# Keeping the FFN activation in PSUM for its first 26 steps: a fused gated-attention and FFN kernel on one core

## The chip, the cores and the metric

The kernel runs on one core of a Trainium2 chip (trn2). The time is device microseconds for one launch, the median of several executions. One execution was also taken with the profiler; its rows stand below. The engines are called as the profile calls them: PE (TensorE matmuls), PEld (its weight loads), DVE (VectorE), ACT (ScalarE), POOL (GpSimd), SP (SyncE, which issues the DMAs).

## The reference

Two parts run one after the other. The first is a gated linear recurrence over 768 time steps, for 4 batches of 8 heads with 48 features each; its output is the input of the second, an FFN over 3072 tokens (384 to 2048 to 384) with a piecewise activation.

```
for t in range(S):
    state = alpha[:, :, t, :, None] * state + einsum('bhd,bhe->bhde', k[:, :, t], v[:, :, t])
    y[:, :, t] = einsum('bhd,bhde->bhe', q[:, :, t], state)
x = y.transpose(0, 2, 1, 3).reshape(B * S, H * D)
h = x @ w_in
g = where(h >= 1, h, where(h <= -1, 0, (h + 1) ** 2 / 4))
out = g @ w_out
```

## The kernel before

**Attention.** The 3072 tokens are cut into 24 chunks of 128. For each chunk, `prepare` loads a, k, q and v and forms scaled queries and keys on DVE with two scans along the tokens (L549, L575), two multiplies (L591, L601; L601 is on POOL for most chunks) and small operations. `attend` runs the chunk's matmuls (L665, L678, L691, L818), updates the state (L720, and L795 on POOL) and writes the chunk's output to `ring` as a high and a low part (`end_chunk`: cast on ACT L842, subtraction on DVE L847).

**FFN.** Three chunks form a group, so there are eight groups of 384 tokens; 2048 hidden features are 16 blocks of 128. One *step* is one block of one group, 128 steps in all. The steps of the first two groups are taken in halves (group 0 blocks 0 to 7, group 1 blocks 0 to 7, group 0 blocks 8 to 15, group 1 blocks 8 to 15), so that the first eight blocks of weights serve two groups before the others are needed. A step's number in that order is its `key`. The very first step is cut in three parts of one chunk each.

A step is `hidden` and then `second`. `hidden` makes nine matmuls (L915) into a PSUM bank `h` of 128x384, then the activation: ACT takes relu(h/2 + 1/2) into the SBUF tile `gf` and squares it there (both L944); DVE takes max(min(gf, 1), h) into `gf` (L955); ACT casts `gf` to the high part `gh[:, 0]` (L961); POOL subtracts that from `gf` to give the low part `gh[:, 1]` (L962). The planner may give that subtraction to DVE instead, at a penalty. `second` makes nine matmuls (L980) from `gh` and the block of `w_out` into three output banks, `LAG` steps behind. For the very last step the subtraction is on DVE.

**Weights.** They are loaded as 64-bit words and decoded into a high and a low part for `w_in` and `w_out`, in units of two blocks: on ACT L367, L375, L420; on DVE L383, L394; on POOL L407, L422 (each with DVE as the second choice). That work falls in the first 145 us. The scratch tile `w` has two buffers. The part for `w_out` is due `LAG` steps after that for `w_in`.

**Order of the work.** Nothing is left to a run-time scheduler: `Plan.order` is a list scheduler that runs before the launch. Each operation has an engine, a written duration, a key (its due time in steps), dependencies and buffers. The scheduler goes forward in planned time; on each engine the operation that can start first goes next, the lower key first among those that can start at the same time. The result is a fixed order on each engine, and an engine that waits for one instruction holds up all behind it. Its PSUM is eight banks: at most two for `h` in planned time, three for the output, the rest for attention. An operation marked `port` may not start on DVE inside a planned `port` operation of POOL, or the other way round; `held` remembers that operation's planned start and end. The lines that do it:

```
        held = {"DVE": (0.0, 0.0), "POOL": (0.0, 0.0)}
                    if port:
                        a, b = held["POOL" if engine == "DVE" else "DVE"]
                        t = b + 0.05 * (engine == "DVE") if a <= t < b else t
            t, o, i = best
            o.start = t
            if o.port:
                held[o.engine] = (o.start, t)
```

In planned gaps of PE in the first 165 us the scheduler puts matmuls on zeros (`fill`, L1051), which do no work of the reference.

Of the kernel before, what the change touches and what calls it, by code (L numbers as in the profile page):

```python
# [30 lines left out]
PLACING = 4.0  # L31
MORE = 2
WARM = 15
LAG = 4.0
FETCH = 12.0
LOAD = 4.0
DECODE = 3.0
# [14 lines left out]
HELP = 4  # L52
SPLIT = 1
NEAR = 0.0


class Buf:
# [20 lines left out]
class Plan:  # L78
# [57 lines left out]
    def order(self):  # L136
        free = {"PE": 1.0, "DVE": 1.0, "ACT": 1.0, "POOL": 4.6, "SP": 0.8}
        slots = {name: [(0.0, -i, None) for i in range(n)] for name, (n, share, _) in self.sizes.items() if share == name}
        live = {name: 0 for name in self.sizes}
        left = {}  # L140
        for i, o in enumerate(self.ops):
            o.rank, o.left = i, len(o.deps)
            for d in o.deps:
                d.next.append(o)
            for b in o.allocs:
                left[b] = [len(b.users), 0.0]
        ready = {}
        for o in self.ops:
            if not o.left:
                self.offer(ready, o)  # L150
        mode, wire, done, freed = None, 0.0, [], 0
        held = {"DVE": (0.0, 0.0), "POOL": (0.0, 0.0)}
        while any(ready.values()):
            best = None
            for engine, waiting in ready.items():
                could = []
                for o, i in waiting:
                    _, _, key, _, port = o.ways[i]
                    t = max(free.get(engine, 0.0), o.ready)
                    need = {}  # L160
                    for b in o.allocs:
                        need[b.pool, b.early] = need.get((b.pool, b.early), 0) + 1
                    if any(
                        len(slots[self.sizes[p][1]]) < n or live[p] + n > self.sizes[p][2 if early else 0]
                        for (p, early), n in need.items()
                    ):
                        continue
                    for (p, _), n in need.items():
                        t = max(t, sorted(slots[self.sizes[p][1]])[n - 1][0])
                    if o.moved > 0:  # L170
                        t = max(t, wire - self.DEPTH)
                    if port:
                        a, b = held["POOL" if engine == "DVE" else "DVE"]

                        t = b + 0.05 * (engine == "DVE") if a <= t < b else t
                    could.append((t, key, o.rank, o, i))
                if not could:
                    continue
                soon = min(c[0] for c in could) + NEAR
                _, _, t, o, i = min((key, rank, t, o, i) for t, key, rank, o, i in could if t <= soon)  # L180
                if best is None or t < best[0]:
                    best = t, o, i
            assert best, "no instruction can go: " + str([(e, o.key, [b.pool for b in o.allocs], {p: len(x) for p, x in slots.items()}) for e, w in ready.items() for o, _ in w][:4])
            t, o, i = best
            for j, way in enumerate(o.ways):
                ready[way[0]].remove((o, j))
            o.engine, o.us, _, o.emit, o.port = o.ways[i]
            o.start = t
            rest = t - free["PE"]
            if o.engine == "PE" and self.REST < rest and 1.0 < t < WARMTH and slots["ps"] and min(slots["ps"])[0] <= free["PE"]:  # L190
                n = int((rest - 0.25) / self.FILL)
                f = Op("PE", n * self.FILL, o.key, lambda n=n: self.fill(n), False, "full", 0)
                f.start, f.end = free["PE"], free["PE"] + f.us
                mode = "full"
                done.append(f)
            if o.engine == "PE" and mode != o.mode:
                t += self.MODE
                mode = o.ends
            t += o.us
            free[o.engine] = t  # L200
            if o.port:
                held[o.engine] = (o.start, t)
            if o.moved > 0:
                wire = max(wire, t) + o.moved / self.RATE
                t = wire + self.LAND
            else:
                t += self.HOP.get(o.engine, 0.08)
            o.end = t
            done.append(o)
            for b in o.allocs:  # L210
                live[b.pool] += 1
                free_at = slots[self.sizes[b.pool][1]]
                taken = min(free_at)
                free_at.remove(taken)
                if taken[2]:
                    o.deps.update(taken[2].users)
            for b in o.uses:
                left[b][0] -= 1
                left[b][1] = max(left[b][1], t)
                if not left[b][0]:  # L220
                    live[b.pool] -= 1
                    freed += 1
                    slots[self.sizes[b.pool][1]].append((left[b][1], freed, b))
            for x in o.next:
                x.left -= 1
                x.ready = max(x.ready, t if x.engine != o.engine or o.moved else free[o.engine])
                if not x.left:
                    self.offer(ready, x)
        assert len(done) >= len(self.ops)
        return done  # L230
# [3 lines left out]
def gated_attention_ffn(ctx: ExitStack, tc: tile.TileContext, q, k, v, alpha, laid, out):  # L234
# [77 lines left out]
    with ExitStack() as main:  # L312
# [589 lines left out]
        def hidden(n, f, key, c0=0, c1=GROUP):  # L902

            c1 = min(c1, groups[n])
            L = (c1 - c0) * CH
            h = bank("ps_h", 2, [P, L])
            gf, gh = buf("fw", "gf", [P, L], 4), buf("fw", "gh", [P, 2, L], 4, F32R)
            xs = [("x", j % (2 * GROUP)) for j in range(first[n] + c0, first[n] + c1)]
            at = slice(span(n).start + c0, span(n).start + c1)

            def product():
                m = 0
                for kt in range(KT):
                    for w, a in ((0, 0), (0, 1), (1, 0)):
                        nc.tensor.matmul(  # L915
                            out=h(),
                            lhsT=win(f, w)[:, kt],
                            rhs=ring[:, at, kt, a, :],
                            start=(m == 0),
                            stop=(m == 3 * KT - 1),  # L920
                        )
                        m += 1


            firsts[:] = [
                plan.op(
                    "PE",
                    (0.529 if c1 - c0 > 1 else 0.7) * (c1 - c0),
                    key,
                    product,  # L930
                    [*xs, ("moved", n), wi[f // NW]],
                    [h],
                    mode="full",
                    after=firsts,
                )
            ]


            w = (c1 - c0) / GROUP
            act = lambda in_, func, scale, bias: plan.op(  # L940
                "ACT",
                0.08 + 0.45 * w,
                key + 0.4,
                lambda: nc.scalar.activation(out=gf(), in_=in_(), func=func, scale=scale, bias=bias),  # L944
                [h, gf] if in_ is gf else [h],
                [gf],
            )

            act(h, AF.Relu, 0.5, half_b)
            act(gf, AF.Square, 1.0, 0.0)  # L950
            plan.op(
                "DVE",
                0.08 + 0.45 * w,
                key + 0.4,
                lambda: nc.vector.scalar_tensor_tensor(  # L955
                    out=gf(), in0=gf(), scalar=1.0, in1=h(), op0=ALU.min, op1=ALU.max
                ),
                [gf, h],
                [gf],
            )  # L960
            plan.op("ACT", 0.08 + 0.41 * w, key + 0.4, lambda: nc.scalar.copy(out=gh()[:, 0], in_=gf()), [gf], [gh])  # L961
            sub = lambda e: e.tensor_tensor(out=gh()[:, 1], in0=gf(), in1=gh()[:, 0].bitcast(F32), op=ALU.subtract)  # L962
            ends = (n, f) == (NG - 1, NF - 1)
            ways = [("POOL", 0.1 + 0.9 * w, lambda: sub(nc.gpsimd), True), ("DVE", 0.08 + 0.45 * w, lambda: sub(nc.vector), True)]
            (e, us, emit, port), other = reversed(ways) if ends else ways
            plan.op(e, us, key + 0.4, emit, [gf, gh], [gh], port=port, other=None if ends else other)
            return gh

        o_ps, seconds, firsts = {}, {}, []
# [310 lines left out]
```

## Time and profile before

| | us |
|---|---|
| median of 3 runs | 522.08 (521.63 to 522.26) |
| profiled execution, its own time | 520.75 |
| span of the profiled execution, first to last instruction | 519.0 |
| mean granted TensorE clock | 0.99 |

The profiled execution's 520.75 us is its span and 1.75 us around it. PE is busy 498.3 us of the span, DVE 315.9, ACT 310.4, POOL 274.9. These are sums over stages with different limits, so the sections that follow read them by stretch. The work of DVE, ACT and POOL is heaviest in the first 145 us.

### The profile page before, as it was taken

Reading aid. Unit: us, or ns where it says so; the run is one execution under the profiler, and the core shown is the slowest. Engines: PE = TensorE matmul, PEld = TensorE weight load, DVE = VectorE, ACT = ScalarE, POOL = GpSimd, SP = SyncE. Lnnn points to the kernel's source line nnn. Section 1 sums busy time; section 2 is a strip of 40 time slices with the busy share of each in tenths; the row PEclk is TensorE's granted clock in tenths of the full one; section 3 lists DMA queues with packets and bytes.
Section 4 is the critical chain, followed back from the end, with each engine's and each line's share of the span. In section 5 each row is a group of like instructions: output and inputs, shape, how many; then the busy total and the mean of one; then the engine's idle time right before and its main releaser. Section 6 shows DMA issues by size and latency. Waiting matters only on the chain.

```text
span 519.0 us, 12190 instructions
## 1 busy us (share of the span) xinstructions
PE 498.3 (96%) x4820; PEld 480.2 (93%) x4820; DVE 315.9 (61%) x566; ACT 310.4 (60%) x607; POOL 274.9 (53%) x287
## 2 busy tenths in 40 slices
PE   9899999697999999999999999999999999999996
PEld 7778889696899999999999999999999999999995
DVE  6999999969696685467276456458358413112112
ACT  3898887665656555556555564556556555555541
POOL 3678887999953454455355354365365332333330
PEclk9999999978999999999999999999999999999999
DMA  8996958112226552454334452453222300001001
GB/s 261 375 348 195 317 168 330 43 57 82 71 70 166 157 163 57 113 135 122 81 115 99 119 147 59 111 128 113 56 53 63 79 29 14 11 3 45 1 1 51
DMA packets 59487, 59.81 MB, mean 115 GB/s; under 512 B 33601, under 2 KB 43297, under 8 KB 59425
## 3 DMA queue, kind: packets, MB, share of 16 engines
q1 hardware_dynamic: 59424, 58.97, 38.4%
q8 instruction: 40, 0.66, 0.5%
q14 instruction: 23, 0.18, 0.1%
HBM read 47.32 MB, written 9.57 MB: 110 GB/s over the span
## 4 chain that ended last, share of the span: by engine, by line
PE 73%; DVE 15%; issue 4%; POOL 3%; ACT 2%; DMA 1%; SPq 0%; DVEq 0%; POOLq 0%
PE ps L915 32%; PE ps L980 32%; PE ps L818 4%; DVE inv L575 2%; PE ps L691 2%; DVE Q L549 2%; PE ps L678 2%; DVE w L394 2%; DVE w L383 2%; DMA wt<-in_laid_w_in 1%; POOL gh L962 1%; DVE gf L955 1%; DVE Q L764 1%; POOL w L407 1%; DVE inv L591 1%
## 5 line engine op out<-in xcount | busy, mean ns | idle before, releaser
L962 POOL TENSOR_TENSOR gh<-gf,gh 128x384 fp32r<-128x384 f32 (+1 forms) x128 | 143.6, 1123 | 167.7 <-ACT gh L961 165.9
L980 PE MATMUL ps<-wt,gh 128*128 128x384 f32 x1152 | 226.3, 341 | 5.1 <-DVE gf L955 4.0
L915 PE MATMUL ps<-ring,wt 128*128 128x384 f32 (+1 forms) x1170 | 226.2, 338 | 1.6 <-DVE inv L575 1.2
L980 PEld LDWEIGHTS ps<-wt,gh 128*128 128x128 f32 x1152 | 202.4, 189 | 7.7 <-DVE gf L955 4.6
L915 PEld LDWEIGHTS ps<-ring,wt 128*128 128x128 f32 x1170 | 205.5, 189 | 2.6 <-ACT gf L944 1.5
L955 DVE SCALAR_TENSOR_TENSOR gf<-gf,ps 128x384 f32<-128x384 f32 (+1 forms) x130 | 70.1, 542 | 161.4 <-ACT gf L944 152.6
L961 ACT CAST gh<-gf 128x384 fp32r<-128x384 f32 (+1 forms) x130 | 65.8, 508 | 96.1 <-DVE gf L955 95.1
L944 ACT ACTIVATE gf<-ps,half_b 128x384 f32<-128x384 f32 (+1 forms) x130 | 74.8, 575 | 75.3 <-PE ps L915 71.9
L944 ACT ACTIVATE gf<-gf 128x384 f32<-128x384 f32 (+1 forms) x130 | 67.6, 520 | 4.0
L795 POOL TENSOR_TENSOR state<-state,last 128x192 f32<-128x192 f32 x20 | 20.1, 1006 | 33.1 <-DVE state L720 30.9
L407 POOL TENSOR_TENSOR w<-w,wt 128x384 int32<-128x384 int32 (+1 forms) x24 | 31.1, 1307 | 11.0 <-DVE w L394 5.1
L575 DVE TENSOR_TENSOR_SCAN inv<-raw,bwd 128x511 f32<-128x511 f32 x17 | 32.5, 1911 | 0.0
L422 POOL TENSOR_TENSOR wt<-w,wt 128x384 fp32r<-128x384 f32 (+1 forms) x25 | 31.3, 1266 | 1.9 <-ACT wt L420 1.7
L601 POOL TENSOR_TENSOR Q<-Q,raw 128x512 f32<-128x512 f32 x18 | 29.9, 1662 | 2.4 <-POOL last L558 1.0
L764 DVE TENSOR_TENSOR Q<-ps,mask 64x256 f32<-64x256 f32 x48 | 20.3, 423 | 15.2 <-ACT other L728 14.3
L818 PE MATMUL ps<-other,both 128*64 128x64 f32 x372 | 27.8, 229 | 0.2 <-DVE other L764 0.2
L818 PE MATMUL ps<-Q,both 128*64 128x64 f32 x372 | 27.9, 229 | 0.0
L818 PEld LDWEIGHTS ps<-Q,both 128*64 128x64 f32 x372 | 24.4, 141 | 2.7 <-issue 1.1
L710 ACT COPY both<-state 48x192 f32<-48x192 f32 x67 | 23.4, 349 | 2.6 <-DVE state L718 0.8
L549 DVE TENSOR_TENSOR_SCAN Q<-raw,fwd 128x512 f32<-128x512 f32 x17 | 24.4, 1434 | 0.8 <-PE ps L818 0.7
L818 PEld LDWEIGHTS ps<-other,both 128*64 128x64 f32 x372 | 24.3, 141 | 0.3 <-issue 0.3
L691 PEld LDWEIGHTS ps<-vt,ks 64*64 64x64 f32 x704 | 13.7, 138 | 9.5 <-ACT ks L668 5.3
(77 smaller groups left out, 411.2 us busy)
## 6 DMA issues: line engine op xcount, KB each, us to landing
both<-in_laid_v_both SPq DMA_DIRECT2D x48, 128.0 KB, 2.8
wt<-in_laid_w_in SPq DMA_DIRECT2D x8, 768.0 KB, 7.9
wt<-in_laid_w_out SPq DMA_DIRECT2D x8, 768.0 KB, 8.3
vt<-in_laid_v SPq DMA_DIRECT2D x24, 192.0 KB, 2.8
out<-ot SPq DMA_DIRECT2D x24, 192.0 KB, 1.9
raw<-in_laid_dim_a SPq DMA_DIRECT2D x17, 256.0 KB, 3.1
raw<-in_laid_dim_k SPq DMA_DIRECT2D x17, 256.0 KB, 3.4
raw<-in_laid_dim_q SPq DMA_DIRECT2D x17, 256.0 KB, 2.6
```

The lines of the kernel that those rows point to most:

```text
L407: add = lambda e, c=c: e.tensor_tensor(out=bits()[:, c], in0=bits()[:, c], in1=word(I32, 0)[:, c], op=ALU.add)
L422: sub = lambda e, c=c: e.tensor_tensor(out=part(1)[:, c], in0=data()[:, c], in1=part(0).bitcast(F32)[:, c], op=ALU.subtract)
L549: lambda: nc.vector.tensor_tensor_scan(flat(Q()), aT(), flat(fwd), 0.0, ALU.mult, ALU.max),
L575: lambda: nc.vector.tensor_tensor_scan(flat(inv())[:, 0:n][:, ::-1], aT()[:, 1 : n + 1][:, ::-1], flat(bwd)[:, 0:n][:, ::-1], bwd[:, G - 1 ...
L601: mul = lambda e: e.tensor_tensor(out=flat(Q()), in0=flat(Q()), in1=qT(), op=ALU.mult)
L818: nc.tensor.matmul(out=ps()[halves[r], to, halves[u]], lhsT=lhsT[:, r, u], rhs=x()[:, g, halves[u]], start=m + u == 0, stop=True, skip_gro ...
L915: nc.tensor.matmul(out=h(), lhsT=win(f, w)[:, kt], rhs=ring[:, at, kt, a, :], start=(m == 0), stop=(m == 3 * KT - 1),)
L944: lambda: nc.scalar.activation(out=gf(), in_=in_(), func=func, scale=scale, bias=bias),
L955: lambda: nc.vector.scalar_tensor_tensor(out=gf(), in0=gf(), scalar=1.0, in1=h(), op0=ALU.min, op1=ALU.max),
L961: plan.op("ACT", 0.08 + 0.41 * w, key + 0.4, lambda: nc.scalar.copy(out=gh()[:, 0], in_=gf()), [gf], [gh])
L962: sub = lambda e: e.tensor_tensor(out=gh()[:, 1], in0=gf(), in1=gh()[:, 0].bitcast(F32), op=ALU.subtract)
L980: nc.tensor.matmul(out=o_ps[seg][t](), lhsT=gh()[:, a, (t - c0) * CH : (t - c0 + 1) * CH], rhs=wout(f, w), start=(f == f0 and i == 0), sto ...
```

## The change

For the steps whose key is below `APART = 26` (the first part-steps of step 0 included) `x` is the PSUM bank `h` itself: DVE's max writes back into `h`, ACT casts out of it, and DVE, with no second choice, subtracts out of it. From step 26 on the chain is as before. `held` keeps the last four `port` operations of each engine instead of the last one, and each is tested. `LAG` goes from 4 to 3, for `second` and for the decoding of `w_out`.

```
-LAG = 4.0
+LAG = 3.0
+APART = 26.0
...
-        held = {"DVE": (0.0, 0.0), "POOL": (0.0, 0.0)}
+        held = {"DVE": [], "POOL": []}
...
-                        a, b = held["POOL" if engine == "DVE" else "DVE"]
-                        t = b + 0.05 * (engine == "DVE") if a <= t < b else t
+                        for a, b in held["POOL" if engine == "DVE" else "DVE"]:
+                            t = b + 0.05 * (engine == "DVE") if a <= t < b else t
...
-                held[o.engine] = (o.start, t)
+                held[o.engine] = [*held[o.engine][-3:], (o.start, t)]
...
+            x = h if key < APART else gf
             plan.op(
                 "DVE", 0.08 + 0.45 * w, key + 0.4,
                 lambda: nc.vector.scalar_tensor_tensor(
-                    out=gf(), in0=gf(), scalar=1.0, in1=h(), op0=ALU.min, op1=ALU.max
+                    out=x(), in0=gf(), scalar=1.0, in1=h(), op0=ALU.min, op1=ALU.max
                 ),
                 [gf, h],
-                [gf],
+                [x],
             )
-            plan.op("ACT", 0.08 + 0.41 * w, key + 0.4, lambda: nc.scalar.copy(out=gh()[:, 0], in_=gf()), [gf], [gh])
-            sub = lambda e: e.tensor_tensor(out=gh()[:, 1], in0=gf(), in1=gh()[:, 0].bitcast(F32), op=ALU.subtract)
+            plan.op("ACT", 0.08 + (0.45 if x is h else 0.41) * w, key + 0.4, lambda: nc.scalar.copy(out=gh()[:, 0], in_=x()), [x], [gh])
+            sub = lambda e: e.tensor_tensor(out=gh()[:, 1], in0=x(), in1=gh()[:, 0].bitcast(F32), op=ALU.subtract)
             ends = (n, f) == (NG - 1, NF - 1)
+            if x is h:
+                plan.op("DVE", 0.08 + 0.45 * w, key + 0.4, lambda: sub(nc.vector), [x, gh], [gh])
+                return gh
             ways = [("POOL", 0.1 + 0.9 * w, lambda: sub(nc.gpsimd), True), ("DVE", 0.08 + 0.45 * w, lambda: sub(nc.vector), True)]
             (e, us, emit, port), other = reversed(ways) if ends else ways
-            plan.op(e, us, key + 0.4, emit, [gf, gh], [gh], port=port, other=None if ends else other)
+            plan.op(e, us, key + 0.4, emit, [x, gh], [gh], port=port, other=None if ends else other)
             return gh
```

## Rows read from the trace of the kernel before

**Rows 1.** Busy time of each engine by stretch, in us from the start of the span: the stretch and its length, then for each engine busy us and the count of instructions, then the mean granted TensorE clock (1.00 is 2.4 GHz, 0.5 is 1.2 GHz), the busy share of the DMA engines and GB/s.

```profile
core 0: us, PE busy (x) PEld busy (x) DVE busy (x) ACT busy (x) POOL busy (x), PEclk, DMA share, GB/s
0.00:20.00 20.00, 18.32 (x274) 15.12 (x275) 15.19 (x34) 10.12 (x22) 9.48 (x23) 1.00 0.91 304
20.00:80.00 60.00, 55.17 (x768) 49.29 (x767) 56.96 (x105) 53.54 (x102) 48.44 (x58) 1.00 0.81 273
80.00:145.00 65.00, 55.78 (x460) 53.69 (x459) 54.35 (x70) 42.17 (x79) 57.23 (x41) 0.92 0.30 103
145.00:165.00 20.00, 19.76 (x198) 19.27 (x198) 15.11 (x27) 12.23 (x26) 8.52 (x11) 1.00 0.44 128
165.00:505.00 340.00, 340.00 (x3077) 334.27 (x3076) 170.65 (x326) 189.67 (x376) 150.19 (x155) 1.00 0.31 81
...
102.00:109.00 7.00, 5.98 (x103) 5.74 (x104) 4.34 (x5) 2.21 (x4) 6.92 (x6) 0.51 0.19 60
...
126.00:129.50 3.50, 3.50 (x13) 3.50 (x13) 3.43 (x6) 2.61 (x6) 3.50 (x3) 0.51 0.93 273
```

**Rows 2.** The order of PE's instructions from 94 to 126 us: start, length, engine, line, operation, names, shape, count, and in brackets the idle time before them and what ended it.

```profile
96.77 1.50 PE L980 MATMUL ps<-wt,gh 128*128 128x384 f32 x7 [1.07 <-POOL gh L962]
98.11 1.74 PE L915 MATMUL ps<-ring,wt 128*128 128x384 f32 x9
103.02 1.10 PE L691 MATMUL ps<-vt,ks 64*64 64x48 f32 x32 [3.18 <-ACT ks L668]
...
118.94 1.74 PE L915 MATMUL ps<-ring,wt 128*128 128x384 f32 x9
120.52 1.21 PE L980 MATMUL ps<-wt,gh 128*128 128x384 f32 x6
125.32 0.78 PE L980 MATMUL ps<-wt,gh 128*128 128x384 f32 x3 [3.60 <-DVE gf L955]
```

**Rows 3.** The chain that ended last, its pieces in order of time between 80 and 145 us: start, length, what. Only the pieces of L962 on POOL and the longer ones of L383, L394, L549 and L558 are shown.

```profile
82.46 1.31 DVE w L383
83.79 1.94 DVE w L394
...
94.81 1.91 POOL gh L962
...
99.94 1.28 POOL gh L962
...
101.30 1.24 POOL last L558
...
103.86 1.71 POOL gh L962
...
116.22 1.97 DVE w L383
...
118.21 1.66 DVE w L394
...
120.33 2.63 DVE Q L549
...
128.56 1.51 DVE w L383
...
136.28 1.72 POOL gh L962
```

**Rows 4.** Groups of POOL's instructions from 80 to 145 us: line, engine, operation, names, shapes, count, then busy us and mean ns of one, then idle time before them.

```profile
L962 POOL TENSOR_TENSOR gh<-gf,gh 128x384 fp32r<-128x384 f32 x16 | 21.8, 1365 | 1.3 <-ACT gh L961 1.3
```

**Rows 5.** The same groups of DVE from 80 to 145 us.

```profile
L394 DVE SCALAR_TENSOR_TENSOR w<-wt,w 128x768 int32<-128x768 int32 x8 | 12.0, 1502 | 0.2
L383 DVE TENSOR_SCALAR w<-w 128x768 int32<-128x768 int32 x8 | 10.7, 1332 | 0.8 <-ACT w L367 0.8
L549 DVE TENSOR_TENSOR_SCAN Q<-raw,fwd 128x512 f32<-128x512 f32 x3 | 6.4, 2140 | 0.0
L575 DVE TENSOR_TENSOR_SCAN inv<-raw,bwd 128x511 f32<-128x511 f32 x3 | 6.2, 2079 | 0.0
```

**Rows 6.** The same groups from 20 to 80 us, two of POOL and then four of DVE.

```profile
L962 POOL TENSOR_TENSOR gh<-gf,gh 128x384 fp32r<-128x384 f32 x6 | 8.2, 1386 | 0.5 <-ACT gh L961 0.4
...
L962 POOL TENSOR_TENSOR gh<-gf,gh 128x128 fp32r<-128x128 f32 x3 | 2.4, 799 | 0.0
...
L575 DVE TENSOR_TENSOR_SCAN inv<-ps,bwd 128x511 f32<-128x511 f32 x5 | 6.4, 1272 | 0.0
L549 DVE TENSOR_TENSOR_SCAN Q<-ps,fwd 128x512 f32<-128x512 f32 x5 | 6.1, 1223 | 0.2
...
L962 DVE TENSOR_TENSOR gh<-gf,gh 128x384 fp32r<-128x384 f32 x1 | 0.8, 804 | 0.2 <-ACT gh L961 0.2
L955 DVE SCALAR_TENSOR_TENSOR gf<-gf,ps 128x128 f32<-128x128 f32 x3 | 0.8, 278 | 0.0
```

**Rows 7.** Single instructions of DVE in order of time, at moments when they ran short: start, length, then as in rows 2. The last one is the subtraction of the very last step.

```profile
101.96 0.55 DVE L383 TENSOR_SCALAR w<-w 128x768 int32<-128x768 int32 x1
...
134.22 0.96 DVE L394 SCALAR_TENSOR_TENSOR w<-wt,w 128x768 int32<-128x768 int32 x1
...
510.00 0.56 DVE L962 TENSOR_TENSOR gh<-gf,gh 128x384 fp32r<-128x384 f32 x1 [0.58 <-ACT gh L961]
```

**Rows 8.** Groups over the whole span, shapes kept apart: operations that read PSUM beside the same kind reading SBUF.

```profile
L961 ACT CAST gh<-gf 128x384 fp32r<-128x384 f32 x127 | 65.0, 513 | 96.1 <-DVE gf L955 95.1 <-DVE raw L546 0.5
...
L847 DVE TENSOR_TENSOR ring<-ps,ring 128x384 fp32r<-128x384 f32 x3 | 1.7, 553 | 0.3 <-ACT ring L842 0.3
L842 ACT CAST ring<-ps 128x384 fp32r<-128x384 f32 x3 | 1.4, 478 | 0.3 <-PE ps L818 0.2
...
L546 DVE MEMSET raw<- 128x4 f32 x17 | 1.1, 62 | 1.0
...
L546 DVE MEMSET ps<- 128x4 f32 x7 | 0.4, 62 | 0.5
```

**Rows 9.** PE's order at the end of the FFN, as in rows 2.

```profile
505.80 1.74 PE L915 MATMUL ps<-ring,wt 128*128 128x384 f32 x9
507.38 3.64 PE L980 MATMUL ps<-wt,gh 128*128 128x384 f32 x20
```

## The prediction

> **What bounds the kernel now.** I read the busy time by stretch first [rows 1]. From 165 to 505 us PE is busy for all 340.00 us at the full granted clock, and nothing in the change touches the amount of PE's work. So the end moves only by what PE loses before 165 us, and by the tail. In 145 to 165 us PE loses 0.24 us. In 80 to 145 us it is busy 55.78 of 65.00 us: 9.2 us are idle. In the same stretch the granted clock is at its lower level (0.51, that is 1.2 GHz) over 102 to 109 and 126 to 129.5 us, each time behind a long idle time of PE. There PE was busy 5.98 and 3.50 us; at 0.51 of the rate that is about 0.49 x 9.48 = 4.6 us of work lost. So 80 to 145 us holds 13.8 us that could in principle come back. In 20 to 80 us PE is idle for 4.8 us, beside filler matmuls that do no work.
>
> Next the waits themselves, in PE's order [rows 2]. Three matter: 1.07 us for a low part from POOL (L962), 3.18 us for an ACT copy (L668), and 3.60 us for a DVE maximum (L955), which is a wait for a PSUM bank. The last two stand just ahead of the two stretches at the lower clock.
>
> Then the chain, to see what made ACT and DVE late [rows 3]. It runs over POOL and DVE: decoding (L383, L394), the scan (L549), and four pieces of POOL's subtraction L962, 1.91 + 1.28 + 1.71 + 1.72 = 6.6 us. POOL is busy 57.23 of these 65 us and DVE 54.35 [rows 1]. In 20 to 80 us it is the other way round: DVE is busy 56.96 of 60 us, POOL 48.44.
>
> Last, single instructions. DVE's decoding takes 0.55 us (L383) and 0.96 us (L394) at moments when it runs short [rows 7], but 1.33 and 1.50 us on the mean of 80 to 145 us [rows 5]. The scan out of PSUM takes 1.22 us each time [rows 6], out of SBUF 2.14 us [rows 5]. DVE instructions that read two SBUF tiles, and some that read one, are held while POOL works; those that read PSUM are not.
>
> **The four port spans.** The scheduler picks the operation that can start earliest over all engines, so planned starts hardly ever go back. A span before the last one of an engine then ends before the time that is tested. The only way back is a PSUM bank offered in the past, after the limit on banks of a kind had held an operation. I cost this edit at nothing; the orders that the other edits give matter more.
>
> **The subtraction moved from POOL to DVE.** It concerns 25 whole subtractions and three parts. One whole one was on DVE already, at 0.80 us [rows 6]; 22 of POOL's started between 20 and 145 us, 16 of them after 80 us [rows 4, 6].
>
> - *POOL, 80 to 145 us.* It loses 21.8 of 57.23 us [rows 1, 4], 38%. On the chain the four pieces of 6.62 us become DVE pieces. No row shows this subtraction out of PSUM; the same operation for the ring does 128x384 in 0.553 us [rows 8], and the one out of SBUF at the quiet end takes 0.56 us [rows 7], so 0.55 us it is. Four of these are 2.2 us: 4.4 us back. Ends: 0, if each new one waits in DVE's order as long as the old one did, and 6.6.
> - *DVE freed from POOL.* The chain's pieces of L383, L394 and L549 exceed the short times by 4.79 - 1.65, 3.60 - 1.92 and 2.63 - 1.22, together 6.2 us [rows 3, 6, 7]. If the delay follows POOL's load, 38% of it goes: 2.4 us back, between 0 and 6.2.
> - *DVE's new work.* After 80 us it is 16 x 0.55 = 8.8 us; DVE has 10.6 us idle there and gets back some of its held time, so beyond what stands on the chain I charge nothing. Before 80 us it is 6 x 0.55 + 3 x 0.28 = 4.1 us (0.278 us is the part-step's maximum [rows 6]), less 0.25 for the one already there: 3.9 us on an engine with 3.0 us idle. Behind each subtraction stand the scans and multiplies of the next chunk, for which PE waits. The cost lies between 0.9 us, if all idle time is filled, and 3.9; I take 3.0.
>
> **The activation in PSUM.** DVE's maximum now writes PSUM. No such row of that size exists; a small memset takes 62 ns into either memory [rows 8]. ACT's cast out of PSUM should be 0.478 instead of 0.513 us [rows 8]: below 1 us over 25 steps, and ACT is not the tightest engine. I cost both at nothing. The Trainium skill ("Perfetto Trace Analysis", section Optimizing Scalar/DVE Operations) gives DVE about 65 ns more of access overhead for PSUM than for SBUF; by that two operations in 28 calls would add some 3.6 us to DVE as an estimate, and the forecast would fall to about no change. The pair 0.553 and 0.56 us above shows no such difference here.
>
> What is not free is the bank. It used to come free after the maximum; now it is held through the cast and the subtraction, 0.48 + 0.55 us and two handovers, about 1.1 us more. The scheduler sees that and will put other matmuls in between, but the real order runs late against the plan, as the 3.60 us wait for a bank shows [rows 2]. I charge 1.1 us for each of two such waits, 2.2 us. Ends: 0, and 16 steps x 1.1 = 17.6.
>
> **The lag.** Three steps in place of four issue the same matmuls in another order, and bring the decoding of `w_out` forward by one step; no instruction or DMA is added to SP's or another queue. At the end the last hidden product ends at 507.54 us and its low part at 510.56 us, 3.0 us later [rows 7, 9]. With three steps, two second products cover that instead of three; 20 matmuls take 3.64 us there, so 18 take some 3.2 us. The cover is just enough: 0. In the early stretch a wait like the 1.07 us one [rows 2] becomes easier to hit, but each low part also comes sooner: 0, at most twice 1.07 us.
>
> **The lower clock.** If a long wait goes or shrinks, so does the slow stretch behind it. I count half of the 4.6 us: 2.3, between 0 and 4.6.
>
> **The sum.** -4.4 - 2.4 - 2.3 + 3.0 + 2.2 = -3.9 us. Against the profiled execution's own 520.75 us (519.0 of span and 1.75 around it) that is 516.85; the median of the runs stands 1.33 us above the profiled one, so the forecast for the median is 518.2 us. Its own range is 514 to 520.5: the ends of the first two gains and of the clock, not all at once. The three runs spread over 0.12%; a change below 0.2% (about 1 us) can't be told from none.
>
> **The rivals.**
>
> *Both long waits go.* Then the 13.8 us of 80 to 145 us return, less 3.0 in front: -10.8, 511.3 us. For it: POOL, the fullest engine of that stretch, loses 38% of its work, and both slow stretches follow waits. Against it: DVE takes over, and the 3.60 us wait is one for a bank.
>
> *The bank is the new wait, and the kernel gets slower.* Place: a first or second product on PE that waits for a bank which DVE's late subtraction holds, in 80 to 145 us. Price: 1.1 us for each step it strikes, and the slow clock stays. The gains left are 4.4 + 2.4 - 3.0 = 3.8 us, so it decides from the fourth step on; at six of the 16 steps it is 6.6 - 3.8 = +2.8, 524.9 us. For it: PE already waited 3.60 us for a bank, and DVE's order has scans of 2 us ahead of such a subtraction. Against it: the scheduler knows of the longer hold.
>
> *DVE becomes the bound and nothing is gained.* 54.35 + 8.8 = 63.2 of 65 us if its held time does not shrink; then POOL's relief is idle time, and 522 us stays. Against it: the 6.2 us of excess above. The Trainium skill, same page and section, says of moving operations between the two that it "might not help", because they share a port; by that this rival would hold. The rows speak only half for it, as the operation moved reads one tile from PSUM and such instructions show no delay [rows 6].
>
> **Chances.** The forecast 0.46, both waits gone 0.17, no change 0.14, the bank 0.23. So faster by over 0.2% 0.63, within 0.2% 0.14, slower 0.23. The range goes to the rivals on both sides: 511 to 524.8 us.
>
> **What would show it.** The step on POOL is right if POOL falls to some 35 us in the stretch that answers to 80 to 145 us and L962 leaves the chain; the relief, if L383 and L394 come down to 0.9 and 1.2 us there; the new subtraction, if it takes 0.55 us. The front is right if the work that PE has done by 80 us is some 3 us behind. The bank shows as PE waits ended by L962 or L955 on DVE. The clock shows in its rows. The steady stretch must stay without idle time. The forecast is wrong if the new order on DVE puts the chunks' scans late, which no row of before can show, or if the longer hold of a bank strikes often.

## The result, and the profile after

The changed kernel takes 512.09 us (511.91 to 512.73) against 522.12 us before in the same comparison: a ratio of 0.9819, 95% interval 0.9806 to 0.9832. That is 10.0 us faster. The forecast was 518.2 us; the measured time lies inside the range, 0.8 us from the rival in which both long waits go (511.3 us). The profiled execution has a span of 510.4 us against 519.0.

Busy time by stretch of the changed kernel; the columns are those of [rows 1].

```profile
20.00:80.00 60.00, 53.96 (x769) 48.63 (x768) 51.77 (x111) 52.49 (x100) 37.99 (x50) 1.00 0.88 299
80.00:145.00 65.00, 63.30 (x531) 61.69 (x530) 52.16 (x94) 47.44 (x92) 42.42 (x34) 1.00 0.27 83
145.00:165.00 20.00, 20.00 (x201) 19.58 (x200) 14.80 (x30) 11.13 (x24) 11.86 (x13) 1.00 0.59 151
165.00:490.00 325.00, 325.00 (x2991) 319.27 (x2990) 162.31 (x309) 184.11 (x365) 137.06 (x148) 1.00 0.31 82
```

In 80 to 145 us PE's idle time fell from 9.2 us [rows 1] to 1.7 us, and the granted clock is 1.00 throughout: both stretches at the lower clock are gone. POOL fell from 57.23 to 42.42 us, not to the 35 us of the forecast: 22 instructions of its decoding (L407, L422) lie in the stretch now, 18 before. DVE fell too, from 54.35 to 52.16 us, although it took over the subtractions. The steady stretch after 165 us is full as before.

How far PE is in the FFN tells where the time went. These rows count the whole-step matmuls of the changed kernel begun by 80 us (first two) and by 145 us (last two); L915 is the first product, L986 the second.

```profile
L915 PE MATMUL ps<-ring,wt 128*128 128x384 f32 x81 | 15.9, 342 | 0.6 <-DVE gh L965 0.6
L986 PE MATMUL ps<-wt,gh 128*128 128x384 f32 x54 | 11.0, 346 | 0.0
...
L915 PE MATMUL ps<-ring,wt 128*128 128x384 f32 x241 | 46.6, 339 | 0.6 <-DVE gh L965 0.6
L986 PE MATMUL ps<-wt,gh 128*128 128x384 f32 x216 | 42.3, 341 | 0.1
```

The same rows of the kernel before:

```profile
L915 PE MATMUL ps<-ring,wt 128*128 128x384 f32 x90 | 17.8, 344 | 1.6 <-DVE inv L575 1.2 <-DVE gf L955 0.4
L980 PE MATMUL ps<-wt,gh 128*128 128x384 f32 x55 | 11.5, 348 | 0.0
...
L915 PE MATMUL ps<-ring,wt 128*128 128x384 f32 x214 | 43.2, 348 | 1.6 <-DVE inv L575 1.2 <-DVE gf L955 0.4
L980 PE MATMUL ps<-wt,gh 128*128 128x384 f32 x189 | 39.3, 352 | 5.1 <-DVE gf L955 4.0 <-POOL gh L962 1.1
```

A product of nine matmuls starts 1.58 us after the one before it [rows 9], so a matmul is worth 0.175 us. The attention matmuls begun by 80 and by 145 us are as many in both kernels. By 80 us the changed kernel is 145 - 135 = 10 matmuls behind, 1.75 us. By 145 us it is 457 - 403 = 54 ahead, 9.5 us. So 80 to 145 us gave 64 matmuls, 11.2 us: 7.5 us less idle time and the 4.6 us of work that the lower clock had cost, less 0.9 us of matmuls on zeros that now lie there. The last matmul ends at 504.42 us instead of 514.30, 9.9 us sooner. The span is only 8.6 us shorter, as it ends 6.0 us after the last matmul instead of 4.7. (The medians are 10.0 us apart because the traced execution of the kernel before was 1.3 us below its median.)

What DVE's instructions cost in 80 to 145 us after the change, to be held against [rows 5]:

```profile
L965 DVE TENSOR_TENSOR gh<-ps,gh 128x384 fp32r<-128x384 f32 x19 | 10.5, 550 | 8.1 <-ACT gh L964 8.1
...
L394 DVE SCALAR_TENSOR_TENSOR w<-wt,w 128x768 int32<-128x768 int32 x8 | 7.6, 953 | 0.1
L383 DVE TENSOR_SCALAR w<-w 128x768 int32<-128x768 int32 x8 | 5.8, 726 | 0.7 <-ACT w L367 0.7
L575 DVE TENSOR_TENSOR_SCAN inv<-raw,bwd 128x511 f32<-128x511 f32 x3 | 3.8, 1275 | 0.0
L549 DVE TENSOR_TENSOR_SCAN Q<-raw,fwd 128x512 f32<-128x512 f32 x3 | 3.8, 1268 | 0.0
```

L394 fell from 1.502 to 0.953 us, L383 from 1.332 to 0.726, the scans from 2.08 and 2.14 to 1.28 and 1.27. Over these four lines the time above the short durations (0.96, 0.55, 1.27 and 1.22 us [rows 6, 7]) was 15.8 us before and is 1.6 us now.

The waits of PE in 20 to 145 us of the changed kernel: engine and line, who ended the wait, us in total, times, the longest.

```profile
PE ps L665 <- DVE inv L591: 4.7, 4, 1.6
...
PE ps L691 <- ACT ks L668: 0.6, 1, 0.6
PE ps L915 <- DVE gh L965: 0.6, 1, 0.6
```

The three waits of [rows 2] are gone. The only one for a bank in the subtraction's hands is 0.6 us, and it comes before 80 us. On the chain that ended last POOL's subtraction is gone from 80 to 145 us; DVE's (L965) has four pieces there, 0.2 us together.

### The profile page after: what moved, and what is told of

The parts are those of the page before. It is cut to its first block, busy times and chain, and to the rows that moved or that the text cites. A ratio compares the mean times of both kernels' runs of the same rounds, so it can differ in the third digit from the quotient of the medians.

```text
span 510.4 us, 12184 instructions
## 1 busy us (share of the span) xinstructions
PE 494.7 (97%) x4836; PEld 477.6 (94%) x4836; DVE 300.9 (59%) x582; ACT 311.5 (61%) x610; POOL 241.7 (47%) x268
## 4 chain that ended last, share of the span: by engine, by line
PE 76%; DVE 10%; POOL 4%; ACT 3%; DMA 2%; issue 2%; SPq 1%; DVEq 0%; POOLq 0%
PE ps L986 34%; PE ps L915 33%; PE ps L818 4%; PE ps L691 2%; PE ps L678 2%; POOL wt L422 2%; DVE inv L575 2%; POOL w L407 2%; DVE Q L549 1%; DVE w L394 1%; DMA wt<-in_laid_w_in 1%; DMA raw<-in_laid_tok_a 1%; DVE ps L958 1%; DVE Q L764 1%; ACT gf L944 1%
## 5 line engine op out<-in xcount | busy, mean ns | idle before, releaser
L915 PE MATMUL ps<-ring,wt 128*128 128x384 f32 (+1 forms) x1170 | 224.2, 336 | 0.6 <-DVE gh L965 0.6
L986 PE MATMUL ps<-wt,gh 128*128 128x384 f32 x1152 | 223.9, 339 | 0.1
L915 PEld LDWEIGHTS ps<-ring,wt 128*128 128x128 f32 x1170 | 204.6, 188 | 1.1 <-DVE gh L965 0.7
L986 PEld LDWEIGHTS ps<-wt,gh 128*128 128x128 f32 x1152 | 201.1, 188 | 1.8 <-POOL wt L422 0.4
L965 POOL TENSOR_TENSOR gh<-gf,gh 128x384 fp32r<-128x384 f32 x101 | 109.7, 1087 | 169.6 <-ACT gh L964 169.5
L958 DVE SCALAR_TENSOR_TENSOR gf<-gf,ps 128x384 f32<-128x384 f32 x102 | 56.2, 551 | 153.2 <-ACT gf L944 150.3
L964 ACT CAST gh<-gf 128x384 fp32r<-128x384 f32 x102 | 52.3, 513 | 66.9 <-DVE gf L958 66.9
L407 POOL TENSOR_TENSOR w<-w,wt 128x384 int32<-128x384 int32 (+1 forms) x26 | 32.7, 1274 | 18.5 <-DVE w L394 15.9
L422 POOL TENSOR_TENSOR wt<-w,wt 128x384 fp32r<-128x384 f32 (+1 forms) x26 | 33.8, 1314 | 12.4 <-ACT wt L420 12.2
L601 POOL TENSOR_TENSOR Q<-Q,raw 128x512 f32<-128x512 f32 x18 | 23.3, 1294 | 3.8 <-DVE inv L567 2.3
L575 DVE TENSOR_TENSOR_SCAN inv<-raw,bwd 128x511 f32<-128x511 f32 x17 | 23.0, 1354 | 0.0
L549 DVE TENSOR_TENSOR_SCAN Q<-raw,fwd 128x512 f32<-128x512 f32 x17 | 20.9, 1229 | 0.2
L965 DVE TENSOR_TENSOR gh<-ps,gh 128x384 fp32r<-128x384 f32 (+1 forms) x28 | 14.5, 522 | 10.7 <-ACT gh L964 10.5
## 6 DMA issues: line engine op xcount, KB each, us to landing
both<-in_laid_v_both SPq DMA_DIRECT2D x48, 128.0 KB, 3.0
```

The costliest lines, as they stand in the source:

```text
L407: add = lambda e, c=c: e.tensor_tensor(out=bits()[:, c], in0=bits()[:, c], in1=word(I32, 0)[:, c], op=ALU.add)
L422: sub = lambda e, c=c: e.tensor_tensor(out=part(1)[:, c], in0=data()[:, c], in1=part(0).bitcast(F32)[:, c], op=ALU.subtract)
L549: lambda: nc.vector.tensor_tensor_scan(flat(Q()), aT(), flat(fwd), 0.0, ALU.mult, ALU.max),
L575: lambda: nc.vector.tensor_tensor_scan(flat(inv())[:, 0:n][:, ::-1], aT()[:, 1 : n + 1][:, ::-1], flat(bwd)[:, 0:n][:, ::-1], bwd[:, G - 1 ...
L915: nc.tensor.matmul(out=h(), lhsT=win(f, w)[:, kt], rhs=ring[:, at, kt, a, :], start=(m == 0), stop=(m == 3 * KT - 1),)
L958: lambda: nc.vector.scalar_tensor_tensor(out=x(), in0=gf(), scalar=1.0, in1=h(), op0=ALU.min, op1=ALU.max),
```

## The experiments

Three theories. **A**: the gain is the subtraction that left POOL, and with it the time for which POOL held DVE. **B**: the gain is the scheduler's better test, which keeps `port` operations apart. **C**: it is the shorter lag. All times are compared with runs of the kernel before on the same chip, so the ratio is what counts.

### One part at a time

**e1**: the activation in PSUM and the subtraction on DVE alone.

```
 LAG = 4.0
+APART = 26.0
+held[o.engine] = [(o.start, t)]        # one span, as before
 (hidden() as in the changed kernel)
```

> The kernel before with the subtraction of the first 26 steps on DVE out of PSUM, and nothing else: the lag stays 4 and one port span is tested. Theory A (the gain is the subtraction that left POOL, and with it the time that DVE is held by POOL): 513 to 515 us, the mean of L394 in 80 to 145 us near 1.0 us. Theory B (the gain is the scheduler's keeping port operations apart, the move alone brings little): 517 us or more, L394 still at 1.3 us or above.

Measured: 513.54 us, ratio 0.9837 (0.9808 to 0.9867). A holds for the time, but its number for DVE does not. (The traced execution took 516.42 us, the longest of five.)

```profile
L394 DVE SCALAR_TENSOR_TENSOR w<-wt,w 128x768 int32<-128x768 int32 x8 | 10.0, 1254 | 0.1
L383 DVE TENSOR_SCALAR w<-w 128x768 int32<-128x768 int32 x8 | 7.8, 974 | 0.1
```

In 80 to 145 us DVE is still held for some 0.3 and 0.4 us of each; over the four lines the time above the short durations is 7.6 us, half of the 15.8. PE does not miss the other half in this stretch. Its whole-step matmuls there:

```profile
L986 PE MATMUL ps<-wt,gh 128*128 128x384 f32 x168 | 32.5, 338 | 0.0
L915 PE MATMUL ps<-ring,wt 128*128 128x384 f32 x156 | 30.3, 338 | 0.4 <-DVE ring L847 0.4
```

They are 324; the same view has 324 for the changed kernel and 260 for the kernel before. What this execution lacks was lost earlier: by 80 us it had begun 107 of them, the changed kernel 135. The last section shows where. The move alone brings most of the gain, with DVE freed by half.

**e2**: four port spans alone.

```
-                held[o.engine] = (o.start, t)
+                held[o.engine] = [*held[o.engine][-3:], (o.start, t)]
 (and the test over all of them)
```

> The kernel before with the test of four port spans alone. Theory A, and the prediction, which costed this edit at nothing: 521 to 523 us. Theory B: 517 us or less, with L383 and L394 near 0.6 and 1.0 us on the mean of 80 to 145 us.

Measured: 522.44 us, ratio 1.0019 (1.0002 to 1.0036). B falls as a theory of the whole. The row of stretch 80 to 145 us, that of PE's filler matmuls and those of DVE's decoding in the same stretch (lines are one lower: L393 is L394, L382 is L383):

```profile
80.00:145.00 65.00, 64.87 (x579) 61.70 (x578) 38.77 (x62) 42.40 (x78) 50.10 (x41) 1.00 0.22 70
```

```profile
L1050 PE MATMUL ps<-zeros 128*128 128x256 bf16 x106 | 12.6, 273 | 0.0
```

```profile
L393 DVE SCALAR_TENSOR_TENSOR w<-wt,w 128x768 int32<-128x768 int32 x8 | 9.9, 1247 | 0.2
L382 DVE TENSOR_SCALAR w<-w 128x768 int32<-128x768 int32 x8 | 6.8, 845 | 8.3 <-ACT w L366 8.3
```

The held time on the four lines falls to 6.3 us, but nothing is won. PE looks full, yet 12.6 us of that is filler on zeros, of which the kernel before has none there, and DVE waits 8.3 us for the decoding on ACT ahead of it. What was held time is now waiting that was planned. POOL still has 15 subtractions there (16.7 us), and the decoding comes no sooner; that POOL's work bounds this order is argued, not shown.

**e3**: `LAG = 3.0` in the kernel before, and nothing else.

> The kernel before with a lag of 3 alone. Theories A and B: 521 to 523 us. Theory C (a shorter lag lets the early stretch run better by itself): 519 us or less.

Measured: 524.99 us, ratio 1.0065 (1.0043 to 1.0087). C falls: the shorter lag costs 0.65% here. That is not the nothing which A and B expected (521 to 523 us) either.

**e4**: the changed kernel with `LAG = 4.0`.

> The changed kernel with the lag back at 4. Theories A and B: 511.5 to 513 us, the lag is worth nothing. Theory C: 514 us or more.

Measured: 510.65 us, ratio 0.9794 (0.9763 to 0.9825): at least as fast as the changed kernel, and below both expected ranges.

### The same order, another place for the subtraction

These two keep the changed kernel's plan and so its order on every engine. Only what the first 26 steps emit differs.

**e5**: the maximum goes to SBUF; ACT's cast and DVE's subtraction read it there.

```
-out=x(), in0=gf(), ...   in_=x()   in0=x()
+out=gf(), in0=gf(), ...  in_=gf()  in0=gf()
```

> The changed kernel with its own order on every engine, but for the first 26 steps the maximum is written to SBUF as before, and ACT's cast and DVE's subtraction read it there: the subtraction stays on DVE and has two SBUF inputs, beside POOL's work. Theory A1 (it is POOL's load that counted): 511 to 513 us, as the changed kernel. Theory A2 (it is the shared way to SBUF of POOL and DVE that counted, which the PSUM source avoids): 514 us or more, the subtraction at 0.7 us or more on the mean of 80 to 145 us and its longest one over 1.5 us.

Measured: 517.61 us, ratio 0.9918 (0.9897 to 0.9938). The time is what A2 expected: with POOL at 43.80 us in 80 to 145 us, about as light as in the changed kernel, more than half of the gain is gone. The subtraction there:

```profile
L965 DVE TENSOR_TENSOR gh<-gf,gh 128x384 fp32r<-128x384 f32 x17 | 15.4, 905 | 6.1 <-ACT gh L964 6.1
```

0.905 us on the mean, the longest 1.71 us, against 0.550 us out of PSUM. But most of the loss comes before this stretch. Whole-step matmuls of e5 begun by 80 us (first two) and those in 80 to 145 us (last two):

```profile
L915 PE MATMUL ps<-ring,wt 128*128 128x384 f32 x69 | 14.5, 360 | 0.0
L986 PE MATMUL ps<-wt,gh 128*128 128x384 f32 x36 | 7.7, 350 | 0.0
...
L986 PE MATMUL ps<-wt,gh 128*128 128x384 f32 x162 | 31.6, 342 | 0.4 <-DVE gh L965 0.4
L915 PE MATMUL ps<-ring,wt 128*128 128x384 f32 x153 | 30.4, 344 | 0.0
```

They are 105 and 315, against 135 and 324 in the changed kernel. So 30 of the 39 are lost before 80 us, where six whole subtractions took 0.81 us on the mean. PE also waited 2.2 us there for inputs of the attention to land, 0.5 us in the changed kernel, so not all of the 30 need come from the edit. How the longer subtraction costs PE time in the front is not shown. Nor does the plan know that this subtraction is a `port` operation; an order made for it was not tried.

**e6**: the same, and POOL subtracts, at the same place in the order.

```
+if x is h: plan.op("DVE", ..., lambda: sub(nc.gpsimd), ...)   # sub reads gf
```

> The changed kernel with its own order, but for the first 26 steps the activation is in SBUF and POOL subtracts, at the same place in the order. Theories A1 and A2: 518 us or more, with POOL above 55 of 65 us in 80 to 145 us and L394 back at 1.3 us or above. If the new order made the gain: 514 us or less.

Measured: 520.14 us, ratio 0.9971 (0.996 to 0.9983). POOL is back at 60.47 of 65 us, L394 at 1.552 us. So in this order POOL's subtraction is worth 0.3%, DVE in place of POOL some 0.5% more, and PSUM in place of SBUF about 1% more. The order was planned for a short subtraction on DVE, so the 0.3% is not the price of an order made for POOL.

### The front, and all steps

**e7**: `x = h if 8 <= key < APART else gf`, the first eight steps as before.

> The changed kernel with the first eight steps as before (subtraction from SBUF, on POOL where the scheduler puts it), steps 8 to 25 as changed. If the new work on DVE costs 3 us in the front, as the prediction has it: 509 to 510.5 us. If it costs nothing there: 511.5 to 513 us. If the front gains from the change too: 513.5 us or more.

Measured: 512.91 us, ratio 0.9836 (0.9817 to 0.9855), not to be told from the changed kernel. The prediction's 3 us for DVE's new work in the front are not there.

**e8**: `APART = 128.0`, `LAG = 4.0`.

> The changed kernel with all 128 steps in PSUM and a lag of 4. PE has no idle time after 165 us, so all theories: as with the lag of 4 and 26 steps, 510 to 511.5 us. If a bank that is held longer costs PE time in the steady stretch: 513 us or more.

Measured: 514.35 us (511.83 to 515.93), ratio 0.9863 (0.982 to 0.9906). The time lies where a cost was expected, but the runs spread widely and the interval overlaps that of e4, so whether the later 102 steps cost anything stays open. The profiled execution has PE busy 324.20 of the 325 us after 165:

```profile
165.00:490.00 325.00, 324.20 (x2985) 318.40 (x2984) 202.78 (x401) 178.90 (x363) 41.44 (x55) 1.00 0.31 83
```

There is no stall for banks worth 2 us in the steady stretch, and POOL's 41.44 us there buy nothing, as PE is full either way.

### The lag and the spans once more, five rounds on one chip

**e9** is the changed kernel, **e10** the same with `LAG = 4.0`, **e11** that with the first eight steps as before, **e12** the changed kernel with one span (`held[o.engine] = [(o.start, t)]`).

> The changed kernel itself, beside the next three on the same chip: 511.5 to 513 us.

> The changed kernel with the lag of 4 once more. Theory D (the shorter lag costs about 1 us at the end, where less work covers the last activation and the last three output writes go out later): 510 to 511.5 us, clear of the kernel beside it, with the last instruction 4.7 to 5.0 us after the last matmul instead of 5.4 or more. If the lag is worth nothing: the same as the kernel beside it within 0.5 us.

> The lag of 4, steps 0 to 7 as in the kernel before and steps 8 to 25 in PSUM. If the front neither gains nor loses by the move: as the lag of 4 with all 26 steps, 510 to 511.5 us. If the move costs DVE 3 us in the front, as the prediction has it: 507.5 to 509 us.

> The changed kernel (lag of 3) with one port span tested instead of four. If the four spans are worth nothing, as the prediction has it: 511.5 to 513 us. If they are worth something once POOL has room (the move alone gave 513.5, the move with four spans and a lag of 4 510.7): 514 us or more, and L394 and L383 longer on the mean of 80 to 145 us.

Measured: e9 512.47 us, ratio 0.9832 (0.981 to 0.9855); e10 510.7, 0.9796 (0.9776 to 0.9815); e11 513.16, 0.9822 (0.9798 to 0.9845); e12 515.2, 0.9871 (0.9853 to 0.989).

The lag of 4 was ahead in both comparisons, by 1.4 and 1.8 us, though the intervals overlap in the first (e4) and touch in the second. The cause given under theory D is shown only in part: in e10's trace the span ends 5.6 us after the last matmul, not the 4.7 to 5.0 that were expected, and in e4's, the same kernel, 4.8; in e9's and in the first one of the changed kernel it is 6.0. So the tail is shorter with a lag of 4 in both pairs, but two executions of one kernel differ there by 0.7 us. Where the rest comes from stays open. e11 shows no gain from leaving the front out; it is rather slower than e10, with intervals that overlap. So the 3 us of the prediction fall a second time.

With the move, one span instead of four costs 2.7 us (e12 against e9; the intervals just touch), and 2.9 us with a lag of 4 (e1 against e4; the intervals overlap). The same two lines of DVE in e12:

```profile
L394 DVE SCALAR_TENSOR_TENSOR w<-wt,w 128x768 int32<-128x768 int32 x8 | 9.8, 1226 | 0.1
...
L383 DVE TENSOR_SCALAR w<-w 128x768 int32<-128x768 int32 x8 | 8.3, 1036 | 1.3 <-ACT w L367 1.2
```

DVE is held again, as in e1: 9.0 us over the four lines, at the same load on POOL (42.91 us). So it is the four spans that free DVE once POOL has room. But the freed time accounts for about half of the 2.7 us at most. PE's whole-step matmuls in 80 to 145 us of e12, and a wait of its front:

```profile
L986 PE MATMUL ps<-wt,gh 128*128 128x384 f32 x162 | 32.3, 341 | 0.5 <-ACT gh L964 0.2 <-DVE gh L965 0.2
L915 PE MATMUL ps<-ring,wt 128*128 128x384 f32 x159 | 31.3, 340 | 0.5 <-DVE gh L965 0.4
...
PE ps L818 <- POOL other L746: 2.0, 1, 2.0
```

They are 321, against 324 in the first trace of the changed kernel and 329 in e9: at most 8 matmuls, 1.4 us, for 7.4 us of held time. The rest is lost outside this stretch. In e12 and in e1 PE waits 2.0 us for POOL (L746) near 40 us, and a stretch at the lower clock follows, shown in the last section; the two traces of the changed kernel have neither there.

The plan itself shows what the test does. This counts, in each planned order, the `port` operations of DVE that are planned to start inside a `port` operation of POOL:

```
kernel before              52 of 119
before, four spans (e2)     0 of 115
move alone (e1)            30 of 115
move, lag of 3 (e12)       30 of 115
changed kernel              0 of 115
```

An operation of DVE was pushed behind POOL's span; then POOL's next operation was placed and replaced the remembered span; when the pushed operation was looked at again, its raw time was tested against the new span alone, and it went into the old one after all.

### Load or reads

What is left of theory A has two halves: POOL's time in its order, and POOL's reading of SBUF beside DVE. **e13** and **e14** put work back on POOL in the changed kernel, at the place of each of the 28 subtractions; nothing waits for it.

```
+e13: nc.gpsimd.tensor_tensor(out=junk3, in0=ident (3 times), in1=mask (3 times), op=ALU.subtract)
+e14: nc.gpsimd.memset(junk, 0.0), twice      # junk is 128x512
```

> The changed kernel in its own order, with one more subtraction of 128x384 on POOL at the place of each of the 28 subtractions; it reads two constant tiles in SBUF, writes a scratch tile, and nobody waits for it. It is work beside the reference's, put in as a load. If POOL's load alone decides (its time in order, or its reads): 517 us or more, L394 at 1.2 us or above on the mean of 80 to 145 us. If what counted was that second products waited for POOL's result: 511.5 to 513.5 us.

> As e13, but with two memsets of 128x512 in place of each extra subtraction: about 1 us of POOL's time that writes SBUF and reads nothing. If POOL's time in its order decides: as e13 within 1.5 us. If its reading of SBUF beside DVE decides: 2 us or more faster than e13, with L394 below 1.1 us on the mean of 80 to 145 us.

Measured: e13 526.2 us, ratio 1.0079 (1.0048 to 1.0111); e14 519.54, 0.996 (0.9931 to 0.9989). POOL is busy 57.52 and 57.43 of 65 us in 80 to 145 us, the same. DVE in that stretch of e13 (lines are two higher: L396 is L394, L385 is L383, L577 and L551 the scans, L541 is L539):

```profile
L396 DVE SCALAR_TENSOR_TENSOR w<-wt,w 128x768 int32<-128x768 int32 x8 | 12.6, 1574 | 0.1
...
L385 DVE TENSOR_SCALAR w<-w 128x768 int32<-128x768 int32 x7 | 5.9, 849 | 0.7 <-ACT w L369 0.7
L577 DVE TENSOR_TENSOR_SCAN inv<-raw,bwd 128x511 f32<-128x511 f32 x2 | 3.9, 1941 | 0.0
```

and of e14:

```profile
L396 DVE SCALAR_TENSOR_TENSOR w<-wt,w 128x768 int32<-128x768 int32 x8 | 8.0, 998 | 0.1
L385 DVE TENSOR_SCALAR w<-w 128x768 int32<-128x768 int32 x8 | 7.7, 962 | 0.7 <-ACT w L369 0.7
L541 DVE TENSOR_SCALAR fwd<-raw 128x4 f32<-128x4 f32 x2 | 2.9, 1444 | 0.0
L577 DVE TENSOR_TENSOR_SCAN inv<-raw,bwd 128x511 f32<-128x511 f32 x2 | 2.5, 1272 | 0.0
```

Both halves count. POOL's work with nothing read costs some 7 us over the changed kernel (0.996 against 0.9819); its reads cost about 6 more (1.0079 against 0.996). The reads are what lengthens the DVE instructions with two SBUF inputs. The 7 us are not POOL's time alone, as the memsets write SBUF and L385 and L541 are held beside them; these two are not separated. (The traced executions, 527.68 and 523.31 us, lie above the medians, so their rows are read for busy time and lengths only.)

## Why the prediction was wrong

It had the direction and the place right, and missed the size: 10.0 us for 3.9. The steps that failed are the terms of the lower clock and of the bank in 80 to 145 us (2.3 us counted and 4.6 measured; 2.2 us charged and nothing measured there), and the four port spans put at nothing, which are worth up to 2.7 us once the subtraction has moved. The last lies in part in the same microseconds, so the three are not to be added. Step by step:

- **PE's losses before 165 us set the end: right.** The 9.5 us by which PE is ahead at 145 us are kept to the last matmul; the steady stretch is full in both. The tail behind it, put at nothing, took back over 1 us in the traced executions.
- **The subtraction's price: right.** 0.550 us out of PSUM, as forecast; DVE's maximum takes 0.557 us into PSUM and 0.551 into SBUF, ACT's cast 0.478 us. The 65 ns more for PSUM that the Trainium skill gives ("Perfetto Trace Analysis", section Optimizing Scalar/DVE Operations) do not show in this pair, 0.550 out of PSUM and 0.56 out of SBUF [rows 7]. On the chain it takes 0.2 us and not 2.2.
- **The lower clock: mis-sized.** I counted half of 4.6 us; all of it came back, as both waits ahead of the two stretches went.
- **The bank: mis-sized.** I charged two waits, 2.2 us, in 80 to 145 us. In the trace of the changed kernel PE has no wait there for a bank that the subtraction holds; one of 0.6 us comes before 80 us. Why the longer hold costs so little is not shown.
- **DVE freed from POOL: the rule was wrong, the term need not be.** I gave back 38% of the held time, POOL's share of busy time that left. On the four lines 15.8 us became 1.6, some 90%. The held time does not follow POOL's load: at 42.91 us of load one span leaves 9.0 us of it (e12), at 42.42 us four spans leave 1.6. The better plan alone left 6.3 (e2). But this is not where the missing time came from, as PE did nearly the same work in 80 to 145 us with 7.6 and 9.0 us of it left (e1, e12). With the clock and the bank as measured the forecast's other terms there give 4.4 + 2.4 + 4.6 = 11.4 us, against 11.2 measured. That 4.4 and 2.4 are each right is not shown.
- **The four port spans at nothing: wrong, and so was the reason.** I argued that planned starts hardly ever go back. An operation that was pushed has a raw time in the past; 52 operations of DVE slipped into spans of POOL that way. Alone the edit brings nothing (e2); with the move it is worth up to 2.7 us (e12), at most 1.4 of them in 80 to 145 us. The prediction took the edits one by one and did not ask what each is worth once another has been made.
- **DVE's new work in the front: mis-sized.** PE is 1.75 us behind at 80 us, not 3.0, and e7 and e11 show that this is not the price of the first eight subtractions: leaving them as before gains nothing. What it is the price of stays open. DVE's busy time there fell from 56.96 to 51.77 us with the subtractions added, so part of it had been held time, and DVE had more room than its busy share said.
- **The lag at nothing: not right.** Alone it costs 0.65% (e3); in the changed kernel 4 was ahead of 3 twice, with intervals that overlap or touch.
- **The rivals.** The first one (both waits gone) had 0.17, and both waits did go. That its time came within 0.8 us is partly luck: it counted 13.8 us back in 80 to 145 us and 3.0 lost in front, where 11.2 and 1.75 were measured. Of DVE as the bound: it speaks with the rule of the Trainium skill on POOL and DVE ("Perfetto Trace Analysis", section Optimizing Scalar/DVE Operations: "might not help"). The trace does not bear this out here, since the operation that moved stopped reading SBUF on both inputs; DVE is at 52.16 of 65 us, not 63.2. e5 shows how much hangs on that: the same move with both inputs in SBUF, in an order not made for it, gives less than half.

The best kernel of the study is the changed one with a lag of 4 (e4, e10): 0.9794 and 0.9796 of the kernel before.

## What to carry to other kernels

When two engines hold each other up, the time that one shows as busy is not its work: read the shortest duration of each line beside its mean. The difference can vanish almost whole once the other engine has room and the order keeps the two apart; it does not go in proportion to the load. But it is worth only what hangs on it: with half of it left, PE did nearly the same work here. Price a wait together with what follows it: the lower clock behind two waits came back whole with them. Moving an operation between the two engines pays most when its new form no longer needs what they share, here by reading its operand from the PSUM bank where it already lay. And an edit that is worth nothing alone (a more honest plan) can be worth something once another has made room, so price edits in the order in which they free the bound.

## What the runs showed of the hardware

Which DVE instructions POOL holds depends on what POOL does. Beside POOL subtractions that read SBUF (e13), DVE's L396, two inputs in SBUF, took 1.574 us and the scan L577 1.941; beside POOL memsets of the same total time (e14) 0.998 and 1.272, about their short durations. DVE instructions with one SBUF input, L385 and L541, were still held beside the memsets: 0.962 us where the short duration is 0.55, and 1.444 us for an operation of 128x4 that took 0.16 us in e13. The Trainium skill says this ("SBUF — State Buffer", section Who interferes with whom): an instruction with two SBUF inputs contends only with a GpSimd instruction that reads SBUF, while the mode in which one input uses both ports contends with any. The first half agrees with these rows. That L385 and L541 run in that mode no run here shows; that they are held beside memsets fits it. DVE's subtraction of 128x384 out of PSUM kept its 0.55 us in e12, e13 and e14 alike.

The lower clock came at another place too when PE's order changed, behind a stretch in which PE was idle for much of the time. In e1 (first two rows) and in e12 (last two), columns as in [rows 1]:

```profile
36.00:42.00 6.00, 3.34 (x50) 2.88 (x49) 5.71 (x11) 4.21 (x11) 4.79 (x6) 1.00 1.03 298
42.00:53.00 11.00, 10.65 (x100) 9.06 (x99) 5.76 (x14) 7.48 (x15) 5.54 (x7) 0.53 0.37 127
...
36.00:40.50 4.50, 1.85 (x18) 1.50 (x16) 4.28 (x8) 3.73 (x8) 3.37 (x4) 1.00 1.04 301
40.50:44.20 3.70, 3.70 (x41) 3.27 (x41) 3.53 (x8) 1.57 (x3) 3.41 (x5) 0.54 0.45 156
```

PE was busy 3.34 of 6.00 us in e1 and 1.85 of 4.50 us in e12, and then the clock was granted at 0.53 and 0.54 on the mean (the lower level for most of the stretch) while PE had work for 10.65 and 3.70 us: 0.47 x 10.65 and 0.46 x 3.70, some 5.0 and 1.7 us lost.
